# A float32 sum of exponentials split into two fp16 parts, and the second head group normed two bursts sooner, in a fused attention and feed-forward kernel

## The chip, the cores and the metric

One core of one Trainium2 chip runs the whole program in one launch. The metric is the device time of that launch in microseconds (us), the median of several runs. A separate profiled execution gives the trace that all durations below come from. Engines are named as the profile names them: PE is TensorE's matrix multiply and PEld its weight load, DVE is VectorE, ACT is ScalarE, POOL is GpSimd, SP is SyncE, whose queue issues most transfers.

## The reference

The inputs are `q`, `k`, `v` of 8 batches x 12 heads x 448 rows x 64 columns, gains `g_q`, `g_k` of 64, a first weight of 768 x 2048, a second of 2048 x 768 and an `alpha` of 2048, all float32.

```python
def rmsnorm(x, g):
    rms = np.sqrt(np.mean(x * x, axis=-1, keepdims=True) + 1e-06)
    return x / rms * g
q_n, k_n = (rmsnorm(q, g_q), rmsnorm(k, g_k))
scores = scale * np.matmul(q_n, k_n.transpose(0, 1, 3, 2))   # scale = 1/8
attn = softmax(scores)                                       # over the keys
x = np.matmul(attn, v)      # heads put side by side: 3584 x 768
h = x @ w_in
g = np.maximum(h, 0.0) + alpha * np.minimum(h, 0.0)
out = g @ w_out             # 3584 x 768, float32
```

## The kernel before

**Groups and tiles.** The 12 heads of a batch are worked in three groups of four; `y` counts the 24 groups, so that `y % 3` is 0, 1, 2 for the first, second and third group of a batch (`G` is 3). The 448 rows are held as 64 partitions x 7 (`J`) for two halves of the heads.

**Norming a group** takes these steps, each on its own engine: `load_qk` (L100, four transfers of 224 KB on SP's queue), `square` (L144, two POOL instructions), `reduce` (L158, two on DVE), `root` (L167, a logarithm and an exponential on ACT), `scale` (L176, two POOL instructions that write `qs` in fp16, four buffers), `turn_dma` (L274, two transposing transfers on SP's queue, from `qs` to `qT` and `kT`, used from `y = 7` on, `TD`), and `turn` (L284), which for these groups is one DVE instruction (L288) that multiplies the transposed `kT` by the gains in place. It therefore waits for the transfer that wrote `kT`.

**Attention.** `score` (L322) and `soft` (L340) make one key tile's scores on PE and their exponentials on ACT. The sum over the keys comes in two ways. For the first two groups of a batch `den` (L376) sums on PE with a matrix of fp16 ones. For the third group, from `y = 8` on (`pre`, `PRE`), `add_up` (L348) adds the seven exponential tiles on POOL into the float32 tile `rden`, six additions that follow one another, and `den_pre` (L383) sums that tile over partitions with float32 matmuls by `ones32` into two banks `dnb` (L389), which DVE copies back (L397). `log_pre` and `invert` turn it into a reciprocal on ACT; `attv` (L412) multiplies by the values into `av` and DVE scales the result into `xT` (L439).

**Feed-forward.** `up` (L473) is six matmuls into a bank `hT`, a scaled copy `ah` on ACT (L494) and a maximum on DVE into `gT` (L498), which also frees the bank. `down` (L500) is sixteen matmuls into `op` and a copy on DVE (L520). `bank` (L442) gives them one of two banks of the pool `psf`, or, where `spare` is set, the only tile of the pool `psa` (tag `acc`), and then the names are `hTa` and `opa`. The same `psa` tile holds `dn` and `av`; the same `psf` banks hold `dnb`.

**Order.** All of it is written out by hand as 69 bursts (`n`). A burst has two to four key tiles, at most one `den` and one `attv`, and then its `gaps`: the `up` and `down` units that a planner has put there by estimated costs. Every engine takes its instructions in the order of the program. These tables place the norming steps of group `y`: `turn_at[y]` the burst of `turn`; from a burst `n` worked out at L605 to L634 come the loads (`n - 5` or so), the squares (end of `n - 2`), the reduces (`jobs[n]`, inside the gaps) and `roots[n + 1] = y`, where `root`, `scale` and `turn_dma` stand (L844 to L858). A `turn` in a burst whose first gap is an `up` is put ahead of all gaps of the burst (L886); otherwise it follows the `down`. `load_qk` of a burst stands at the burst's start, ahead of everything else. A new tile waits until the last reader of the tile that had its buffer is done; `nat` has six buffers, two for each group.

| burst | tiles of scores | sum and values | gaps | start of its scores, us |
|---|---|---|---|---|
| 24 | (7,6) (8,0) | - | `up` 12, 13, 14 of batch 1 | 102.17 |
| 25 | (8,1) (8,2) (8,3) | `den` of 6, 7 | a `down`, `up` 15 | 106.19 |
| 27 | (9,1) (9,2) | - | a `down` | 119.14 |
| 28 | (9,3) to (9,6) | `den_pre`, `attv` of 8 | two `down` | 122.35 |
| 31 | (10,4) (10,5) | - | `up` 3 to 7 of batch 2 | 140.93 |
| 35 | (12,1) (12,2) | - | `up` 14, 15, a `down` | 166.19 |
| 36 | (12,3) to (12,6) | `den_pre`, `attv` of 11 | two `down` | 172.07 |

Bursts 39, 47 and 55 stand to groups 15, 18 and 21 as burst 31 stands to group 12.

Of the kernel before, what the change touches and what calls it, by code (L numbers as in the profile page):

```python
# [9 lines left out]
FP32 = mybir.dt.float32  # L10
FP16 = mybir.dt.float16
AF = mybir.ActivationFunctionType
ALU = mybir.AluOpType
# [8 lines left out]
def kernel(  # L22
# [12 lines left out]
    nc = tc.nc  # L35

    B, H, S, D = q.shape
# [4 lines left out]
    G = HH // 2  # L42
# [4 lines left out]
    NG = B * G  # L47
    FB = DF // 4
    TD = min(7, NG)
    EB = 3  # L50
    EARLY = 3 * G
    PRE = 3 * G - 1
    assert G == 3

    cst = ctx.enter_context(tc.tile_pool(name="cst", bufs=1))
    ld = ctx.enter_context(tc.tile_pool(name="ld", bufs=2))
# [18 lines left out]
    nc.vector.memset(epsb, RMS_EPS)  # L75
    ones = cst.tile([128, 64], FP16, name="ones", tag="ones")
    nc.vector.memset(ones, 1.0)
    ones32 = cst.tile([128, 64], FP32, name="ones32", tag="ones32")
    nc.vector.memset(ones32, 1.0)
    ident = cst.tile([128, 128], FP16, name="ident", tag="ident")  # L80
    make_identity(nc, ident)
    ident32 = cst.tile([32, 32], FP32, name="ident32", tag="ident32")
# [13 lines left out]
    nat, sqs, qs, ss_t, rr_t, qkT, vt, xT = {}, {}, {}, {}, {}, {}, {}, {}  # L96
# [187 lines left out]
    def turn(y):  # L284

        if y >= TD:
            t = qkT[y, "k"].rearrange("p j g c -> p (j g c)")
            nc.vector.tensor_scalar(  # L288
                out=t, in0=t, scalar1=gain[:, 0:1], scalar2=None, op0=ALU.mult
            )  # L290
            return
        if y <= G:
            ps = [psf.tile([128, 512], FP32, name="tps", tag="mm") for _ in "qk"]
        else:
            ps2 = psa.tile([128, 2, 512], FP32, name="tps2", tag="acc")
            ps = [ps2[:, 0], ps2[:, 1]]
        tps = [
            t[:, : S].bitcast(FP16).rearrange("p (j c) -> p j c", j=J) for t in ps
        ]
        for tp, nm in zip(tps, "qk"):  # L300
            for j in range(J):
                nc.tensor.transpose(
                    tp[:, j, :], qs[y, nm][:, j].rearrange("p h d -> p (h d)"), ident
                )
        for tp, nm in zip(tps, "qk"):
            t = att.tile([128, J, 2, 64], FP16, name=f"{nm}T", tag=f"{nm}T", bufs=4)
            o = t.rearrange("p j g c -> p j (g c)")
            if nm == "q":
                nc.vector.tensor_copy(out=o, in_=tp)
            else:  # L310
                nc.vector.tensor_scalar(
                    out=o, in0=tp, scalar1=gain[:, 0:1], scalar2=None, op0=ALU.mult
                )
            qkT[y, nm] = t


    expT, rden, scs = {}, {}, {}

    def pre(ys):
        return len(ys) == 1 and ys[0] >= PRE and ys[0] % G == G - 1  # L320
# [27 lines left out]
    def add_up(y, j):  # L348
# [6 lines left out]
        s = rden[y,]  # L355
        nc.gpsimd.tensor_add(out=s, in0=e[:, 0] if j == 1 else s, in1=e[:, j])  # L356

    def over_keys(accs, ys, weights):

        m = 64 if len(ys) == 1 and ys[0] < EARLY else 32  # L360
        if len(ys) == 2:
            heads = [(y, par, 0) for y in ys for par in range(2)]
        else:
            heads = [(ys[0], par, c) for par in range(2) for c in range(64 // m)]
        for j in range(J):
            for h, (y, par, c) in enumerate(heads):
                for g in range(2):
                    nc.tensor.matmul(  # L368
                        out=accs[g][ds(m * h, m), :S],
                        lhsT=weights(g, y, par, ts(c, m), j),  # L370
                        rhs=expT[y][ds(64 * g, 64), j, par, :],
                        start=(j == 0),
                        stop=(j == J - 1),
                    )
# [8 lines left out]
    def den_pre(ys):  # L383
        y = ys[0]
        m = 64 if y < EARLY else 32
        accs = [psf.tile([128, 512], FP32, name="dnb", tag="mm") for _ in range(2)]
        for h in range(128 // m):
            for g in range(2):
                nc.tensor.matmul(  # L389
                    out=accs[g][ds(m * h, m), :S],  # L390
                    lhsT=ones32[ds(64 * g, 64), :m],
                    rhs=rden[ys][ds(64 * g, 64), h * m // 64, :],
                    start=True,
                    stop=True,
                )
        for g in range(2):
            nc.vector.tensor_copy(out=rden[ys][:, g], in_=accs[g][:, :S])  # L397

# [134 lines left out]
    def spin(count, wide=True):  # L533

        ps = psf.tile([128, 512], FP32, name="spin", tag="mm")
        for _ in range(count):
            nc.tensor.matmul(
                out=ps[:, :S], lhsT=idle32[:, :128] if wide else ident,
                rhs=idle32 if wide else idle, start=True, stop=True,
            )  # L540
# [4 lines left out]
    bursts, dens, avs, first_in, last_in = [], {}, {}, {}, {}  # L545
    den_at, av_at, split = {}, {}, {}
# [4 lines left out]
    m = 0  # L551
    while m < NG * J or steps:
        n = len(bursts)
        while steps:
            ys, values = steps[0]
# [18 lines left out]
        while len(bursts[n]) < limit and m < NG * J:  # L574
            y, j = divmod(m, J)
# [13 lines left out]
    def at(n, f, *a):  # L589
        prep.setdefault(max(int(n), 0), []).append((f, a))  # L590

    def after(n, f, *a):
        post.setdefault(max(int(n), 0), []).append((f, a))

    turn_at = {
        y: max(n for n in range(first_in[y]) if y >= TD or n not in dens)
        for y in range(1, NG)
    }
    turn_at[2], turn_at[G] = 5, av_at[0]
    turn_at.update(  # L600
        (y, den_at[y - 2] - pre((y - 2,))) for y in range(TD, NG) if y % G == 1
    )
    turns = {n: y for y, n in turn_at.items()}
    jobs = {}
    for y in range(G, NG):  # L605

        early = y < G + 2
        if early:
            n = turn_at[y - 1] + 1
        elif y == G + 2:  # L610
            n = den_at[G - 1]
        elif y == 2 * G:
            n = turn_at[y] - 4
        elif y % G == 1:
            n = den_at[y - 4] - 1 - pre((y - 2,))
        elif y % G:
            n = den_at[y - G] - pre((y - G,))
        else:
            n = av_at[y - 4]
        if y in (3 * G - 1, 3 * G):  # L620

            after(den_at[G] - (y < 3 * G), load_qk, y)
        else:
            at(n - (6 if early or y % G == G - 1 and pre((y - G,)) else 3 if y == 2 * G else 4 if y < 3 * G else 5), load_qk, y)
        for nm in "qk":
            if y != 2 * G:
                after(n - 2 - (y % G == G - 1 and pre((y - G,))), square, y, nm)
            if early:
                after(n, reduce, y, nm, (0, 1) if (y, nm) == (G, "k") else None)
            else:  # L630
                jobs.setdefault(n + (y == G + 2 and nm == "k"), []).append((reduce, (y, nm)))
        if y == 3 * G:
            after(n, *jobs[n].pop()[:1], y, "k")
        roots[n + 1 + (y in (G + 2, 3 * G))] = y  # L634
# [31 lines left out]
    gaps = [[] for _ in range(NB)]  # L666
    for b in range(B - 1):
        lo, hi = av_at[G * b + G - 1], av_at[G * b + 2 * G - 1]
        ups, old, new = (list(u) for u in periods[b])
        mlp = sum(u[0] for u in ups + old + new)  # L670
        stop = hi
# [62 lines left out]
    both, full, lo, hi = slice(0, 2), slice(0, J), slice(0, K0), slice(K0, J)  # L734
    for h in range(2):
        part_square("q", slice(h, h + 1), full, nc.scalar)
    for h in range(2):
# [13 lines left out]
        out=gain, in0=cols[:, NF : NF + 1], in1=cols[:, NF + 1 : NF + 2]  # L751
# [30 lines left out]
    for n in range(NB):  # L782
# [41 lines left out]
        if sums:  # L824
            den_pre(dens[n])
            attv(avs[n], 0, False, (log_pre, invert))
        elif n in dens and not lead:
            den(dens[n])
# [15 lines left out]
        if n in roots:  # L844
            y = roots[n]
# [21 lines left out]
        spare_at, clock = [], 0.0  # L867
# [15 lines left out]
        if turned and not ups_first and turns[n] >= TD:  # L883
            jobs.setdefault(n, []).append((turn, (turns[n],)))
        elif turned:
            turn(turns[n])  # L886
        for k, (f, a) in enumerate(gaps[n]):
            spare = k in spare_at
            if f is down:
                down(*a, jobs.pop(n, ()), spare)  # L890
            else:
                f(*a, spare)
                done += 1
                if n in jobs and not (lead and done < 5) and (
                    n < av_at[2 * G - 1] or done % 2
                ):
                    g, c = jobs[n].pop(0)
                    g(*c)
                    if not jobs[n]:
                        del jobs[n]  # L900
                while late and done == late[0][0]:
                    _, g, c = late.pop(0)
                    g(*c)
        if not gaps[n] and n in turns and turns[n] >= G:
            if n < den_at[0]:
                spin(1)
            turn(turns[n])
# [41 lines left out]
```

## Time and profile before

| what | value |
|---|---|
| median of 3 runs | 427.19 us (427.19 to 427.2) |
| the profiled execution | 427.42 us |
| its span, first to last instruction | 425.6 us |
| PE busy | 413.7 us, 97% of the span |
| ACT, POOL, DVE busy | 275.3, 239.4, 222.4 us (65%, 56%, 52%) |
| granted TensorE clock | full (1.0) over the span |
| transfers | 53.36 MB, 125 GB/s on average |

The profiled execution lies 0.23 us above the median, and 1.8 us of its time lie outside the span. A PE that is 97% busy leaves few places where it waits, so most of the time that PE gains or loses shows in the end; what the other engines do counts where PE comes to wait for it.

### The profile page before, as it was taken

What the parts mean: (1) busy time and instruction counts of PE and PEld (TensorE: products, weight loads), DVE (VectorE), ACT (ScalarE), POOL (GpSimd) and SP (SyncE); (2) the same over time, 40 slices, a digit from 0 to 9 for tenths busy, and PEclk for the clock granted to TensorE, in tenths of its full rate; (3) what the DMA queues carried; (4) which work ended last, traced back from release to release, by engine and by line L of the source; (5) the groups of instructions that cost most, each with busy time, mean ns of one, the idle gap of its engine ahead of it and who ended that gap; (6) DMA issues with size and microseconds to landing.
All of it is one profiled execution on the core that took longest, in us unless ns stands there. A gap on an engine that the chain in (4) does not pass through costs nothing.

```text
span 425.6 us, 11138 instructions
## 1 busy us (share of the span) xinstructions
PE 413.7 (97%) x4755; PEld 216.5 (51%) x4755; DVE 222.4 (52%) x331; ACT 275.3 (65%) x384; POOL 239.4 (56%) x173
## 2 busy tenths in 40 slices
PE   7889999999999999999999999999999999999996
PEld 3344454544455454544555545554555445555554
DVE  4875964456454636636564545647453343343421
ACT  5898887778856686578846677668847575332200
POOL 6789993494997299373984479482973009000000
PEclk9999999999999999999999999999999999999999
DMA  8999999999538965568455963545333500111033
GB/s 199 242 240 224 204 195 204 204 195 238 117 73 131 210 102 126 85 158 168 97 104 109 187 148 106 105 103 126 62 55 85 104 2 22 39 37 39 18 76 75
DMA packets 68529, 53.36 MB, mean 125 GB/s; under 512 B 35568, under 2 KB 68480, under 8 KB 68480
## 3 DMA queue, kind: packets, MB, share of 16 engines
q1 hardware_dynamic: 53680, 39.73, 42.5%
q0 software_dynamic: 13984, 11.81, 18.5%
q10 hardware_dynamic: 816, 1.11, 1.0%
q8 instruction: 37, 0.61, 0.6%
q14 instruction: 12, 0.10, 0.1%
HBM read 45.62 MB, written 11.01 MB: 133 GB/s over the span
## 4 chain that ended last, share of the span: by engine, by line
PE 86%; ACT 5%; DVE 4%; POOL 2%; issue 1%; ACTq 1%; POOLq 0%
PE op L508 29%; PE hT L454 21%; PE hTa L454 9%; PE sc L329 8%; PE opa L508 6%; PE av L368 5%; PE dn L368 3%; ACT expT L343 2%; PE avb L368 2%; PE dnb L389 2%; ACT ah L494 2%; DVE gT L498 1%; POOL sq L155 1%; DVE ss L163 1%; ACTq L108 1%
## 5 line engine op out<-in xcount | busy, mean ns | idle before, releaser
L343 ACT ACTIVATE expT<-sc,expb 128x896 f16<-128x896 f32 x168 | 161.3, 1003 | 42.8 <-PE sc L329 42.6
L508 PE MATMUL op<-w_out_sb,gT 128*128 128x384 f16 (+1 forms) x752 | 125.8, 323 | 0.5 <-DVE gT L498 0.5
L508 PEld LDWEIGHTS <-gT 128*128 128x128 f16 x912 | 86.0, 98 | 64.7 <-issue 11.8
L454 PE MATMUL hT<-xT,w_in_sb 128*128 128x448 f16 x552 | 114.7, 353 | 0.8 <-DVE gT L498 0.5
L179 POOL TENSOR_TENSOR qs<-nat,rr 128x896 f16<-128x896 f32 x41 | 68.4, 1690 | 82.4 <-issue 45.6
L454 PEld LDWEIGHTS <-w_in_sb 128*128 128x128 f16 x768 | 73.2, 98 | 73.8 <-issue 9.4
L494 ACT ACTIVATE ah<-hT,cols 128x448 f16<-128x448 f32 x91 | 57.4, 632 | 46.5 <-PE hT L454 45.6
L498 DVE TENSOR_TENSOR gT<-hT,ah 128x448 f16<-128x448 f32 x92 | 57.3, 623 | 50.7 <-ACT ah L494 49.8
L155 POOL TENSOR_TENSOR sq<-nat 128x896 f32<-128x896 f32 (+1 forms) x47 | 75.5, 1625 | 7.9 <-DMA nat<-in_q_dram 7.3
L520 DVE COPY osb<-op 128x384 f32<-128x384 f32 (+1 forms) x47 | 25.7, 548 | 69.3 <-PE op L508 68.9
L329 PE MATMUL sc<-qT,kT 64*32 64x448 f16 (+1 forms) x1092 | 54.0, 356 | 4.4 <-ACT expT L343 2.2
L356 POOL TENSOR_TENSOR rden<-rden,expT 128x896 f32<-128x896 f32 x30 | 56.8, 1895 | 2.4
L163 DVE TENSOR_REDUCE ss<-sq 128x14 f32<-128x896 f32 (+1 forms) x48 | 48.9, 1039 | 1.9 <-POOL sq L155 1.8
L454 PE MATMUL hTa<-xT,w_in_sb 128*128 128x448 f16 x204 | 44.1, 352 | 0.0
L494 ACT ACTIVATE ah<-hTa,cols 128x448 f16<-128x448 f32 x34 | 21.6, 634 | 21.0 <-PE hTa L454 20.9
L329 PEld LDWEIGHTS <-kT 64*32 64x32 f16 (+1 forms) x1092 | 17.0, 93 | 35.7 <-issue 29.3
L498 DVE TENSOR_TENSOR gT<-hTa,ah 128x448 f16<-128x448 f32 x34 | 21.2, 624 | 19.6 <-ACT ah L494 18.9
L439 DVE TENSOR_TENSOR xT<-av,rden 128x896 f16<-128x896 f32 x16 | 17.5, 1091 | 21.5 <-ACT rden L410 15.4
L368 PEld LDWEIGHTS <-vt 64*32 64x32 f16 (+1 forms) x1260 | 21.4, 94 | 12.7 <-issue 2.5
L508 PE MATMUL opa<-w_out_sb,gT 128*128 128x384 f16 x160 | 27.7, 326 | 0.0
L368 PE MATMUL av<-expT,vt 64*32 64x448 f16 (+1 forms) x812 | 26.6, 349 | 0.0
L356 POOL TENSOR_TENSOR rden<-expT 128x896 f32<-128x896 f16 x6 | 11.3, 1878 | 20.9 <-ACT expT L343 20.9
(67 smaller groups left out, 215.8 us busy)
## 6 DMA issues: line engine op xcount, KB each, us to landing
out_dram<-osb SPq DMA_DIRECT2D x109, 96.0 KB, 2.2
nat<-in_q_dram SPq DMA_DIRECT2D x46, 224.0 KB, 4.3
nat<-in_k_dram SPq DMA_DIRECT2D x46, 224.0 KB, 4.8
vt<-in_v_dram POOLq DMA_DIRECT2D x16, 336.0 KB, 5.9
w_in_sb<-in_moe_w_in_dram POOLq DMA_DIRECT2D x12, 256.0 KB, 7.2
w_out_sb<-in_moe_w_out_dram POOLq DMA_DIRECT2D x4, 768.0 KB, 11.1
nat<-in_q_dram ACTq DMA_DIRECT2D x2, 224.0 KB, 4.3
nat<-in_k_dram ACTq DMA_DIRECT2D x2, 224.0 KB, 5.7
```

The source lines that it names most:

```text
L155: nc.gpsimd.tensor_mul(out=sqf[:, c], in0=src[:, c], in1=src[:, c])
L163: nc.vector.tensor_reduce(out=o[:, c], in_=sqs[y, nm][:, c], axis=AXIS_X, op=ALU.add)
L179: eng.tensor_mul(out=t.rearrange("p j h d -> p h j d"), in0=nat[y, nm], in1=rr_t[y][:, "qk".index(nm)].unsqueeze(3).broadcast_to((128, 2, ...
L329: nc.tensor.matmul(out=sc[ds(64 * g + m * c, m), par, :S].rearrange("p (j c) -> p j c", j=J), lhsT=kT[ds(64 * par, 64), j, g, ts(c, m)], r ...
L343: nc.scalar.activation(out=expT[y][:, j], in_=scs[y, j][:, :, :S], func=AF.Exp, scale=QK_SCALE, bias=expb[:, 0:1],)
L356: nc.gpsimd.tensor_add(out=s, in0=e[:, 0] if j == 1 else s, in1=e[:, j])
L368: nc.tensor.matmul(out=accs[g][ds(m * h, m), :S], lhsT=weights(g, y, par, ts(c, m), j), rhs=expT[y][ds(64 * g, 64), j, par, :], start=(j = ...
L454: nc.tensor.matmul(out=hT[:, :S], lhsT=w_in_sb[:, g * G + i, ts(ft, 128)], rhs=xT[b][:, g, i, :], start=(i == 0 and g == 0), stop=(i == G ...
L494: nc.scalar.activation(out=ah, in_=hT[:, :S], func=AF.Copy, scale=alpha_sb[:, ft : ft + 1])
L498: nc.vector.tensor_max(out=gT[:, ft, ds((b & 1) * S, S)], in0=hT[:, :S], in1=ah)
L508: nc.tensor.matmul(out=ops[c][:, :PW], lhsT=gT[:, ft, ts(t, 128)], rhs=w_out_sb[:, ft, ds(oh * OH + c * PW, PW)], start=(ft == 0), stop=(f ...
L520: nc.vector.tensor_copy(out=o[:, ts(c, PW)], in_=ops[c][:, :PW])
```

## The change

Two things change.

**The sum.** `split_sum` is new. In the burst ahead of `den_pre`, after the first unit of the gaps, ACT writes an eighth of the float32 sum as fp16 (`hi`), and DVE writes the rest, an eighth of the sum less `hi`, as fp16 (`lo`). Both take buffers of `qs`. `den_pre` then runs two passes of fp16 matmuls by a matrix of eights, one over `hi`, one over `lo`, into the same banks. The last unit of the gaps in that burst, and no other, is made spare.

**The norming.** For the second group of a batch from `y = 13` on, loads, squares, reduces, root, scale and transposing transfers stand two bursts sooner. The turns of the groups from `y = 10` on move as well.

| group | root, scale, `turn_dma`: before, after | `turn`: before, after |
|---|---|---|
| 10 | 24, 24 | 27, 24 |
| 11 | 28, 28 | 31, 30 |
| 12 | 29, 29 | 33, 31 |
| 13 | 32, 30 | 35, 32 |

The loads of group 13 move from the start of burst 26 to that of burst 24. Groups 14 to 22 repeat this, eight bursts on for each batch: 14, 17, 20 as 11; 15, 18, 21 as 12; 16, 19, 22 as 13. Group 23 keeps its place.

```diff
-    ones32 = cst.tile([128, 64], FP32, name="ones32", tag="ones32")
-    nc.vector.memset(ones32, 1.0)
+    eights = cst.tile([128, 64], FP16, name="eights", tag="eights")
+    nc.vector.memset(eights, 8.0)
...
+    def split_sum(y):
+
+        s = rden[y,]
+        hi, lo = (
+            ld.tile([128, 2, S], FP16, name="qs", tag="qs", bufs=4) for _ in range(2)
+        )
+        nc.scalar.activation(out=hi, in_=s, func=AF.Copy, scale=0.125)
+        nc.vector.scalar_tensor_tensor(
+            out=lo, in0=s, scalar=0.125, in1=hi, op0=ALU.mult, op1=ALU.subtract
+        )
+        halves[y] = (hi, lo)
...
-        for h in range(128 // m):
-            for g in range(2):
-                nc.tensor.matmul(
-                    out=accs[g][ds(m * h, m), :S],
-                    lhsT=ones32[ds(64 * g, 64), :m],
-                    rhs=rden[ys][ds(64 * g, 64), h * m // 64, :],
-                    start=True,
-                    stop=True,
-                )
+        for n, part in enumerate(halves[y]):
+            for h in range(128 // m):
+                for g in range(2):
+                    nc.tensor.matmul(
+                        out=accs[g][ds(m * h, m), :S],
+                        lhsT=eights[ds(64 * g, 64), :m],
+                        rhs=part[ds(64 * g, 64), h * m // 64, :],
+                        start=(n == 0),
+                        stop=(n == 1),
+                    )
...
-    turn_at.update(
-        (y, den_at[y - 2] - pre((y - 2,))) for y in range(TD, NG) if y % G == 1
-    )
+    turn_at.update((y, den_at[y - 2]) for y in range(TD, NG) if y % G == 1)
+    for y in range(PRE + 1, NG):
+        if y - 2 >= PRE and y % G == 1:
+            turn_at[y] = den_at[y - 4] - 1
+        elif y - 1 > PRE and y % G == 0:
+            turn_at[y] = turn_at[y - 1]
+            turn_at[y - 1] -= 1
...
-            n = den_at[y - 4] - 1 - pre((y - 2,))
+            n = den_at[y - 4] - 1 - pre((y - 2,)) - 2 * pre((y - 5,))
...
+        if n + 1 in dens and pre(dens[n + 1]) and gaps[n]:
+            spare_at = [len(gaps[n]) - 1]
         for k, (f, a) in enumerate(gaps[n]):
...
+            if k == 0 and n + 1 in dens and pre(dens[n + 1]):
+                split_sum(dens[n + 1][0])
```

More of the change, by code (lines that the diff above doesn't have):

```diff
@@ L314, in turn @@
             qkT[y, nm] = t
-    expT, rden, scs = {}, {}, {}
+    expT, rden, scs, halves = {}, {}, {}, {}
     def pre(ys):
```

## The prediction

> **What bounds the kernel now.** I read the page's busy shares first, then the chain that ended last, then the waits around the two moved things. PE is the bound and the chain is almost all PE:
>
> ```profile
> PE 413.7 (97%) x4755; PEld 216.5 (51%) x4755; DVE 222.4 (52%) x331; ACT 275.3 (65%) x384; POOL 239.4 (56%) x173
> ...
> PE 86%; ACT 5%; DVE 4%; POOL 2%; issue 1%; ACTq 1%; POOLq 0%
> ```
>
> So whatever takes PE's time or makes PE wait shows in the end. The groups of `den_pre` (by line and shape) and the waits of its tile say what the sum costs now:
>
> ```profile
> L389 PE MATMUL dnb<-rden,ones 64*32 64x448 f32 x80 | 6.9, 547 | 0.0
> ...
>   DVE osb L520: 1.5, 5
>   POOL rden L356: 0.4, 1
> ```
>
> Each of 44 float32 matmuls stands as two records. PE waited 1.5 us there for `osb` copies that freed the banks, and once 0.4 us for POOL's last addition. That is all the sum can give back. The other half of the change moves `turn`, a DVE instruction that waits for a transfer. Groups 10 and 12 show what that transfer stands behind. First group 10: POOL's `scale`, SP's queue, then DVE and PE (timelines of each, starts in us):
>
> ```profile
> 104.40 3.33 POOL L179 TENSOR_TENSOR qs<-nat,rr 128x896 f16<-128x896 f32 x2 [6.32 <-issue]
> ...
> 96.13 1.28 SPq L108 DMA_DIRECT2D nat<-in_k_dram  x2
> 97.53 1.25 SPq L277 DMA_TRANSPOSE qT<-qs  x1
> 98.87 1.24 SPq L277 DMA_TRANSPOSE kT<-qs  x1
> ...
> 106.12 1.24 SPq L277 DMA_TRANSPOSE qT<-qs  x1
> 107.77 1.22 SPq L277 DMA_TRANSPOSE kT<-qs  x1
> ...
> 103.34 0.61 DVE L498 TENSOR_TENSOR gT<-hT,ah 128x448 f16<-128x448 f32 x1
> 104.83 0.62 DVE L498 TENSOR_TENSOR gT<-hT,ah 128x448 f16<-128x448 f32 x1 [0.87 <-ACT ah L494]
> 106.25 0.62 DVE L498 TENSOR_TENSOR gT<-hTa,ah 128x448 f16<-128x448 f32 x1 [0.80 <-ACT ah L494]
> ...
> 106.93 1.52 PE L368 MATMUL dn<-expT,ones 64*32 64x448 f16 x56 [0.17 <-DVE gT L498]
> ```
>
> The reader sees that `qs` of group 10 is ready at 106.08 (q) and 107.73 (k), its transposes go out at once, and PE's `dn` starts when DVE has freed the `psa` tile that `hTa` held. Then group 12, burst 31, SP, DVE and PE again:
>
> ```profile
> 142.21 1.24 SPq L277 DMA_TRANSPOSE kT<-qs  x1
> ...
> DMA to landing us min/median/max: 4.1/4.2/4.3
> ...
> 143.45 0.62 DVE L498 TENSOR_TENSOR gT<-hT,ah 128x448 f16<-128x448 f32 x1 [0.76 <-ACT ah L494]
> ...
> 144.85 2.43 PE L454 MATMUL hT<-xT,w_in_sb 128*128 128x448 f16 x12
> ```
>
> Its `kT` lands at 142.21 + 4.3 = 146.5, after burst 31 has begun (140.93).
>
> **Stall A, group 10.** Its root, scale and transposes stay in burst 24, but its `turn` now stands in burst 24 too, ahead of that burst's three `gT` (`up` 12, 13, 14), because the first gap is an `up`. DVE takes its queue in order, so after 103.96 it waits for `kT`. And group 13's loads now stand ahead of group 10's transposes on SP: they take over group 10's `nat` buffers, so the q loads wait until 106.08, are issued in 1.34, the k loads wait until 107.73 and end about 109.05. The transposes follow at 109.1 and 110.45 (spacing 1.34, as at 97.53 and 98.87). Landing: the pair at 97.53 also stood right behind four loads and took 4.2 to 4.7; the bounds of the trace for other pairs are 2.9 (nothing ahead) and 5.8 (group 8). I take 4.3: 114.75. Then `turn`, 0.44 to 1.12 by the L288 rows, the longer where POOL adds beside it; take 0.7. Then two `gT` of 0.62, the second of which frees `hTa`: 116.7. Queued behind the waiting instruction are three `gT`; PE waits for the second at `dn`, having done `up` 12 to 14 and two scores. Stall: 116.8 - 106.93 = 9.9; bounds 8.2 (landing 2.9, turn 0.44) to 11.7 (5.8, 1.12).
>
> **The clock after stall A.** The trace has no idle PE that long in its middle. At its start PE runs at half pace (a weight load each 0.37) from 1.61 to 6.25; at its end 3.8 us of idle show full clock:
>
> ```profile
> 5.88 0.15 PEld L537 LDWEIGHTS <-ident 128*128 128x128 f16 x1 [0.22 <-issue]
> 6.25 0.67 PEld L537 LDWEIGHTS <-ident 128*128 128x128 f16 x4 [0.22 <-issue]
> ...
> 421.80:425.60 3.80, 0.00 (x1) 0.00 (x0) 0.36 (x1) 0.00 (x0) 0.00 (x0) 1.00 0.24 52
> ```
>
> So the cost lies between 0 and 2.3 (half of 4.64). I take 1.8, nearer the start's row, since 9.9 is far over 3.8. [...]
>
> **Stall B, groups 12, 15, 18, 21.** Their transposes keep their place; their `turn` comes two bursts sooner, ahead of the five `up` of bursts 31, 39, 47, 55. DVE then waits until `kT` has landed, runs 0.44 (POOL rests there) and only then the first `gT` (0.62), which frees the bank for the fourth `up` (PE adds 0.06). Burst 31: 146.5 + 0.5 + 0.62 + 0.06 = 147.68 against 144.85, so 2.8. Likewise with `kT` issued at 191.19, 239.68, 288.94 and landing 3.6, 4.4, 3.8 later, and the fourth `up` at 194.13, 243.05, 292.33: 1.85, 2.2, 1.6. Sum 8.4; bounds 6.4 and 11.0 with landings 0.5 either way and a `turn` of up to 0.6 more at POOL's side. Groups 11, 14, 17, 20 follow a `down`, or land before their burst (14: 182.79 + 2.9 = 185.7 against 186.45), and cost nothing. Groups 13, 16, 19, 22 have their transposes two bursts sooner, behind the earlier ones (13: issued about 146.0, landed 150.3, wanted at 149.9 + 2.8): nothing, covered by stall B itself; were B absent, some 1 us each.
>
> **The sum.** Float32 takes, from the last score to `av`, 0.81 in group 8 without its wait, 0.95 in groups 11 to 20 with the wait for `osb`, and 1.50 in the last. Two fp16 passes take 0.39 (as 8 score matmuls 64*64) or 0.44 (16 of 64*32; 72 such run in 2.0, 173.40 to 175.41). New on ACT: `hi`, 0.95 by the L401 row, hidden in its idle ahead of `den_pre` (3.9 us at 221.12). New on DVE: `lo`, no such row; 0.87 (fp16 L288, with POOL) to 1.09 (float32 L179); take 1.09, its input being float32.
> - Groups 14, 20 (two `down`): both covered, the spare bank ends the wait: -0.5 each.
> - Groups 11, 17: `split_sum` sits between two `up`. `ah` 15 moves behind `hi` (169.6 to 170.55), `gT` 15 behind `lo` (170.6 to 171.7), done 172.3. The `down` starts 0.25 sooner but its sixteenth matmul needs `gT` 15 at 171.57: 0.8 lost, 0.25 and 0.5 gained: about 0.
> - Group 8: one `down`, so `lo` stands behind the `osb` copy: `av` 2.0 after the scores instead of 1.31, and the spare tile is still being copied, 0.2: +0.9.
> - Group 23: the third `up` loses its spare bank (0.4), `den_pre` falls from 1.50 to 0.44: -0.65.
>
> Together -0.65; bounds -4.4 (all of the float32 excess, 3.6, and every wait, 0.8, gone) and +2 (the loss of group 8 in 11 and 17 as well).
>
> **Sum.** 427.42 + 9.9 + 1.8 + 8.4 - 0.65 = 446.9 for a profiled execution, 0.2 less as a median (427.19 against 427.42): 446.6.
>
> **Rivals.**
> 1. Only stall A: B is hidden, if the transposes of group 12 leave SP at least 3 us sooner. SP's row is packed from 131.76 to 144.8, which speaks against. 427.2 + 9.9 + 1.8 - 0.65 = 438.3.
> 2. Only stall B: group 10's `turn` finds `kT` in time. `qs` ends at 107.73, so it can't. 434.9.
> 3. The change does what its words say, with neither stall: the float32 excess and the waits go. 427.2 - 0.65 to -4.4: 423 to 426.5, faster. The place is the DVE queue in burst 24, the price what A and B sum to; it decides if that is under 0.65. Against it: the data for `kT` does not exist at 103.96.
> 4. Worse: SP's queue, held up by loads that wait for POOL, delays later loads and squares by a burst in each batch, 5 x 2 us more: 457. The free time of POOL (8.8 us before `scale` at 149.45) speaks against.
>
> **How the numbers follow.** Main case 0.80, rival 1 0.08, rival 2 0.03, rival 3 0.06, rival 4 0.03. Low ends together: 427.2 + 8.2 + 0 + 6.4 - 4.4 = 437.4; high ends: 427.2 + 11.7 + 2.3 + 11.0 + 2 = 454.2. They will not all fall together, so 437 to 453, which takes in rival 1. About 0.2% (0.85 us) can be told from no change: faster 0.06, same 0.02, slower 0.92.
>
> **What would show it.** Right: a DVE wait of some 10 us at L288 in burst 24, PE idle before `dn` L368 of about 10 us, PEclk below 1.0 after it; four PE waits of 1.5 to 3 us at `hT` put down to DVE; `dnb` near 0.45 a group. Wrong: PE's idle before `dn` under 1 us, or no PE wait in bursts 31, 39, 47, 55.

## The result and the profile after

The changed kernel takes 447.78 us, the median of 6 runs (446.36 to 449.74), against 427.19 before (427.17 to 428.08): a ratio of 1.0481, 95% interval 1.0455 to 1.0507. The prediction was 446.6, range 437 to 453. The profiled execution took 448.82 with a span of 446.9.

The page of the changed kernel first: busy shares, granted clock in 40 slices of 11.2 us, and the chain that ended last.

```profile
PE 415.6 (93%) x4755; PEld 214.9 (48%) x4755; DVE 225.3 (50%) x337; ACT 280.2 (63%) x390; POOL 243.0 (54%) x173
...
PEclk9899999999699999999999969999999999999999
...
PE 74%; ACT 6%; DVE 5%; issue 5%; DMA 5%; POOL 4%; SPq 1%; ACTq 1%; POOLq 0%; DVEq 0%
```

PE is busy 415.6 us against 413.7, but its share of the chain is 74% against 86%: most of the 21.3 us of new span is time in which PE waits. The clock has two dips in its middle, slices 11 and 24, and one at its start, slice 2, ahead of anything that the change moves. The waits of the changed kernel name what came last (total us, times, longest):

```profile
DVE kT L288 <- DMA kT<-qs: 23.4, 5, 9.9
...
PE dn L380 <- DVE gT L511: 9.4, 1, 9.4
PE hT L467 <- DVE gT L511: 7.7, 7, 3.1
...
PE dnb L402 <- DVE qs L365: 1.0, 1, 1.0
```

Five times DVE stood at `turn` (L288) for a transfer of `kT`; once that held `dn`, four times an `up`. The last row is PE waiting for `lo` (L365) in group 8. Stall A, the timelines of SP, DVE and PE and the clock (the column before the last two of a windows row):

```profile
106.84 1.25 SPq L108 DMA_DIRECT2D nat<-in_q_dram  x2
108.48 1.25 SPq L108 DMA_DIRECT2D nat<-in_k_dram  x2
109.83 1.25 SPq L277 DMA_TRANSPOSE qT<-qs  x1
111.13 1.30 SPq L277 DMA_TRANSPOSE kT<-qs  x1
...
114.56 1.21 DVE L288 TENSOR_SCALAR kT<-kT,gain 128x896 f16<-128x896 f16 x1 [9.87 <-DMA kT<-qs]
...
116.88 2.81 PE L380 MATMUL dn<-expT,ones 64*32 64x448 f16 x56 [9.40 <-DVE gT L511]
...
112.00:116.00 4.00, 0.00 (x0) 0.00 (x0) 1.45 (x2) 0.00 (x0) 3.44 (x2) 0.50 0.61 112
116.00:120.00 4.00, 3.12 (x60) 1.23 (x59) 1.36 (x3) 0.00 (x0) 0.00 (x0) 0.50 0.01 4
```

Group 13's loads stand ahead of group 10's transposes, `turn` waits 9.87 us, and `dn` starts after 9.40 us of idle; the clock is then half. The fence below is burst 47, DVE, PE and clock:

```profile
260.32 0.45 DVE L288 TENSOR_SCALAR kT<-kT,gain 128x896 f16<-128x896 f16 x1 [4.71 <-DMA kT<-qs]
...
261.36 4.64 PE L467 MATMUL hT<-xT,w_in_sb 128*128 128x448 f16 x12 [3.06 <-DVE gT L511]
...
262.00:264.00 2.00, 2.00 (x7) 0.81 (x6) 0.36 (x1) 0.21 (x1) 0.00 (x0) 0.50 0.63 123
264.00:266.00 2.00, 2.00 (x14) 0.59 (x20) 0.62 (x1) 0.43 (x1) 0.00 (x0) 0.50 0.99 253
```

The idle is 3.06 us, and then twelve matmuls take 4.64 where twelve such took 2.43 before: the clock fell here too.

To place every microsecond I subtract, burst by burst, the start of the burst's first score matmul in the trace of before from that in another trace, and take the steps of this difference. Each row holds the steps that belong to one cause, in us; the columns after the first are experiments told below (sooner = the schedule of the change).

| place | changed | float sum, sooner | group 10 back | groups 12-21 back | both back | split only |
|---|---|---|---|---|---|---|
| 24 to 26, stall A | 10.92 | 10.64 | 0.00 | 11.78 | 0.01 | 0.01 |
| 28, 29, sum of group 8 | 0.74 | 0.00 | 6.11 | 0.75 | 6.07 | 6.25 |
| 32, turn of group 12 | 1.69 | 2.19 | 0.00 | 0.00 | 0.00 | 0.00 |
| 36, 37, sum of group 11 | 0.24 | 0.00 | 0.24 | 0.25 | 0.27 | 0.63 |
| 40, turn of group 15 | 1.56 | 1.68 | 1.92 | 0.00 | 0.00 | 0.00 |
| 45, sum of group 14 | -0.61 | 0.00 | -0.61 | -0.61 | -0.61 | -0.08 |
| 48, 49, turn of group 18 | 5.86 | 2.43 | 2.72 | -0.19 | -0.19 | 0.00 |
| 52, 53, sum of group 17 | 0.24 | 0.00 | 0.24 | 0.25 | 0.26 | 0.63 |
| 56, turn of group 21 | 1.16 | 1.34 | 1.01 | 0.00 | 0.00 | 0.00 |
| 61, sum of group 20 | -0.61 | 0.00 | -0.61 | -0.61 | -0.61 | -0.61 |
| after 66, sum of group 23 | -0.38 | 0.00 | -0.39 | -0.37 | -0.39 | -0.37 |

The changed column sums to 20.8. A step of +0.94 in its first 17 us, ahead of anything that the change moves, and -0.4 in bursts 20 and 33, which "float sum, sooner" shows too, make it the 21.3 of the spans. The +0.94 goes with the clock dip of slice 2, which the profiled executions of before, "group 10 back" and "split only" do not have, so it is no part of the change. The profiled execution of "both back" has two such dips in its first 26 us, together +1.88.

### The profile page after: what moved, and what is told of

Read it like the earlier page. It is cut to its first block, busy times and chain, and to the rows that moved or that the text cites. A ratio compares the mean times of both kernels' runs of the same rounds, so it can differ in the third digit from the quotient of the medians.

```text
span 446.9 us, 11155 instructions
## 1 busy us (share of the span) xinstructions
PE 415.6 (93%) x4755; PEld 214.9 (48%) x4755; DVE 225.3 (50%) x337; ACT 280.2 (63%) x390; POOL 243.0 (54%) x173
## 4 chain that ended last, share of the span: by engine, by line
PE 74%; ACT 6%; DVE 5%; issue 5%; DMA 5%; POOL 4%; SPq 1%; ACTq 1%; POOLq 0%; DVEq 0%
PE op L521 23%; PE hT L467 17%; PE opa L521 8%; PE sc L329 7%; PE hTa L467 6%; PE av L380 5%; DMA kT<-qs 5%; POOL qs L179 3%; PE dn L380 3%; ACT expT L343 3%; PE avb L380 2%; DVE gT L511 1%; ACT ah L507 1%; DVE osb L533 1%; PE spin L550 1%
## 5 line engine op out<-in xcount | busy, mean ns | idle before, releaser
L467 PE MATMUL hT<-xT,w_in_sb 128*128 128x448 f16 x558 | 118.8, 358 | 7.7 <-DVE gT L511 7.7
L467 PEld LDWEIGHTS <-w_in_sb 128*128 128x128 f16 x768 | 73.6, 99 | 83.5 <-issue 20.8
L521 PE MATMUL op<-w_out_sb,gT 128*128 128x384 f16 (+1 forms) x656 | 109.7, 323 | 0.0
L155 POOL TENSOR_TENSOR sq<-nat 128x896 f32<-128x896 f32 (+1 forms) x47 | 78.6, 1691 | 10.3 <-DMA nat<-in_q_dram 4.3
L533 DVE COPY osb<-op 128x384 f32<-128x384 f32 (+1 forms) x41 | 22.4, 546 | 61.4 <-PE op L521 61.4
L521 PE MATMUL opa<-w_out_sb,gT 128*128 128x384 f16 x256 | 44.6, 326 | 1.7 <-DVE gT L511 1.6
L467 PE MATMUL hTa<-xT,w_in_sb 128*128 128x448 f16 x198 | 42.8, 352 | 0.0
L329 PEld LDWEIGHTS <-kT 64*32 64x32 f16 (+1 forms) x1092 | 16.1, 93 | 36.7 <-issue 30.4
L380 PEld LDWEIGHTS <-vt 64*32 64x32 f16 (+1 forms) x1260 | 19.5, 93 | 13.1 <-issue 2.8
L380 PE MATMUL dn<-expT,ones 64*32 64x448 f16 (+1 forms) x504 | 16.4, 374 | 9.6 <-DVE gT L511 9.4
```

The costliest lines, as they stand in the source:

```text
L155: nc.gpsimd.tensor_mul(out=sqf[:, c], in0=src[:, c], in1=src[:, c])
L329: nc.tensor.matmul(out=sc[ds(64 * g + m * c, m), par, :S].rearrange("p (j c) -> p j c", j=J), lhsT=kT[ds(64 * par, 64), j, g, ts(c, m)], r ...
L380: nc.tensor.matmul(out=accs[g][ds(m * h, m), :S], lhsT=weights(g, y, par, ts(c, m), j), rhs=expT[y][ds(64 * g, 64), j, par, :], start=(j = ...
L467: nc.tensor.matmul(out=hT[:, :S], lhsT=w_in_sb[:, g * G + i, ts(ft, 128)], rhs=xT[b][:, g, i, :], start=(i == 0 and g == 0), stop=(i == G ...
L521: nc.tensor.matmul(out=ops[c][:, :PW], lhsT=gT[:, ft, ts(t, 128)], rhs=w_out_sb[:, ft, ds(oh * OH + c * PW, PW)], start=(ft == 0), stop=(f ...
L533: nc.vector.tensor_copy(out=o[:, ts(c, PW)], in_=ops[c][:, :PW])
```

## The experiments

The theory was that stall A, stall B and the sum are three separate prices that add up. The rivals: one of the stalls is all of it; the split alone is a gain (rival 3); SP's queue is the cause. Four kernels undo the parts.

**Group 10's turn alone back.** The edit, ahead of where `turns` is made from `turn_at`:

```diff
+    turn_at[10] = 27
     turns = {n: y for y, n in turn_at.items()}
```

> The changed kernel with the turn of group 10 alone back in burst 27, where it stood before; its transposes, all other turns and the split sum stay as changed. Theory (stall A and stall B are separate and add): the start of burst 26 no longer comes 10.9 us late, so 447.8 - 10.9 = 436.9, 436 to 438.2; full clock from 108 to 124 us, but the four waits of bursts 31, 39, 47 and 55 unchanged (together about 10 us with the clock after burst 47). Rival, A is all of it and the other waits only follow from it: 426.5 to 428. Rival, the late transposes of group 10 cost wherever the turn stands: over 440, with a wait of 3 us or more at dn or at the scores of group 10.

Measured: 437.83 us (437.25 to 440.26), ratio 1.0245 (1.0221 to 1.0269). The number is near the theory's, but the table says that the theory is wrong: stall A is gone (0.00), burst 32 lost its stall as well, burst 47 costs 2.7 and not 5.9, and 6.1 us have appeared in group 8, which cost 0.74 in the changed kernel. These terms hang together: while PE loses its time in group 8, SP's queue goes on, so that `kT` of group 12 is issued at 145.05, 1.9 us ahead of burst 31 (146.96); in the changed kernel it is issued at 153.86, 0.5 us after burst 31 has begun (153.31). A total that fits is no proof of its terms.

**The turns of groups 12, 15, 18 and 21 alone back.**

```diff
+    for y in range(12, 22, 3):
+        turn_at[y] += 2
     turns = {n: y for y, n in turn_at.items()}
```

> The changed kernel with the turns of groups 12, 15, 18 and 21 alone two bursts later, in bursts 33, 41, 49 and 57 as before; group 10 and the split sum stay as changed. Theory with the clock: the four idles (1.52, 1.40, 3.06, 1.00 = 7.0 us) and the lower clock after burst 47 (about 2.8 us) go, 447.8 - 9.8 = 438.0, and the granted clock is 1.0 after 130 us. Theory without the clock (the slow stretch after burst 47 has another cause): 440.8, with the clock still down near 260 us. My prediction said for this case that the sooner transposes of groups 13, 16, 19 and 22 then cost some 1 us each: 442. Rival, only B matters: 426 to 428.

Measured: 438.76 us (437.83 to 439.38), ratio 1.0254 (1.0238 to 1.027). All four stalls are 0, and no clock dip is left after stall A's (the twelve `hT` matmuls of burst 47 take 2.43 us). This is the theory with the clock: the median is 9.0 below the changed kernel's, more than the 7.0 of plain idle. The 9.8 expected is missed by about what stall A takes more in this trace, 11.78 against 10.92, after the same idle of 9.40. The sooner transposes of groups 13, 16, 19 and 22, for which the prediction had some 1 us each in this case, cost nothing.

**Both back (e3_both_back), and the split alone (e4_split_only).** The first takes the two edits above together. The second takes neither: it has the whole schedule of before (its `turn_at` and its load bursts), so that only the split is left of the change:

```diff
-    turn_at.update((y, den_at[y - 2]) for y in range(TD, NG) if y % G == 1)
-    for y in range(PRE + 1, NG):
-        ...
+    turn_at.update(
+        (y, den_at[y - 2] - pre((y - 2,))) for y in range(TD, NG) if y % G == 1
+    )
...
-            n = den_at[y - 4] - 1 - pre((y - 2,)) - 2 * pre((y - 5,))
+            n = den_at[y - 4] - 1 - pre((y - 2,))
```

> The changed kernel with both of these undone: the turn of group 10 in burst 27, those of groups 12, 15, 18 and 21 in bursts 33, 41, 49 and 57; groups 11, 13, 14, 16 and so on are still normed and turned sooner, and the sum is split. Theory: what is left is the split sum, +0.74 (group 8), +0.24 each (11, 17), -0.61 each (14, 20) and -0.38 (23) = -0.4, so 426.8, 426 to 427.6. The prediction's remark on groups 13, 16, 19 and 22 (some 1 us each once stall B is absent): 430.8. Rival 3 (the float32 excess and its waits all go): 423 to 424.

> The split sum alone: every load, root, transpose and turn stands in the burst where it stood before, only the float32 sum is split in two fp16 parts as in the change. Theory: -0.4 by the steps seen in the changed kernel's trace (my prediction's sum: -0.65), so 426.5 to 427. Rival 3: 423 to 424, if the 3.6 us of float32 excess all lie on the path. Rival, slower: group 8's and groups 11's and 17's losses without the gains, 428 to 428.5. Also tells whether the sooner norming is worth anything by itself, beside the kernel with both turns back.

Measured: 431.26 us (429.18 to 433.63), ratio 1.0071 (1.0051 to 1.0091), and 433.37 us (432.88 to 434.07), ratio 1.0131 (1.0116 to 1.0146). Every version of the theory falls, and rival 3 too: without the stalls the split is no gain, it is 3.4 and 5.5 us slower than the runs of before beside it (427.86), and the one large step, 6.1 to 6.2, stands in group 8. That 431.26 lies near the 430.8 of the prediction's remark on groups 13, 16, 19 and 22 is chance: no step in the table is theirs. (The profiled execution of "both back", 433.63, is the slowest of its six.) The split alone, POOL, ACT, DVE, PE and clock there, and last POOL and ACT of the changed kernel:

```profile
112.74 9.80 POOL L356 TENSOR_TENSOR rden<-rden,expT 128x896 f32<-128x896 f32 x5
122.49 3.46 POOL L155 TENSOR_TENSOR sq<-nat 128x896 f32<-128x896 f32 x2
...
122.57 0.95 ACT L364 ACTIVATE qs<-rden 128x896 f16<-128x896 f32 x1 [1.26 <-POOL rden L356]
...
122.94 1.49 DVE L288 TENSOR_SCALAR kT<-kT,gain 128x896 f16<-128x896 f16 x1
124.34 2.56 DVE L365 SCALAR_TENSOR_TENSOR qs<-rden,qs 128x896 f16<-128x896 f32 x1
...
123.57 0.38 PE L402 MATMUL dnb<-qs,eights 64*64 64x448 f16 x4 [0.65 <-ACT qs L364]
126.96 0.59 PE L402 MATMUL dnb<-qs,eights 64*64 64x448 f16 x4 [3.00 <-DVE qs L365]
...
130.97 6.26 PE L521 MATMUL op<-w_out_sb,gT 128*128 128x384 f16 x32
...
126.00:130.00 4.00, 3.04 (x32) 1.56 (x31) 2.06 (x3) 1.13 (x2) 1.26 (x2) 0.50 0.71 101
...
125.95 5.82 POOL L356 TENSOR_TENSOR rden<-rden,expT 128x896 f32<-128x896 f32 x3 [2.65 <-ACT expT L343]
...
133.03 0.95 ACT L364 ACTIVATE qs<-rden 128x896 f16<-128x896 f32 x1
```

Group 10's `turn` stands in burst 27 again, ahead of `lo`, and both run beside POOL's squares of group 12: `turn` takes 1.49 and `lo` 2.56, where they take 0.44 and 1.08 with POOL at rest. PE waits 0.65 and 3.00, the clock halves, and 32 `op` matmuls take 6.26 us against the 5.38 of before. In the changed kernel group 8 pays only 0.97 of waiting. One reason is that `turn` has left this burst. The other is POOL: here its additions for group 8 end at 122.54, just as PE ends its scores (122.92), and `hi` waits for them. In the changed kernel PE stood in stall A and POOL caught up, so that the additions end at 131.77 and `hi` is made at 133.03, ahead of PE's `dnb` at 134.69. No run takes the second reason alone. So the parts don't add: what makes stall A is also what keeps the split cheap.

**The sooner schedule alone**, with the float32 sum of before in `den_pre`, no `split_sum` and no unit made spare for it, tests the same from the other side:

```diff
-        for n, part in enumerate(halves[y]):
-            for h in range(128 // m):
-                ...
+        for h in range(128 // m):
+            for g in range(2):
+                nc.tensor.matmul(
+                    out=accs[g][ds(m * h, m), :S],
+                    lhsT=ones32[ds(64 * g, 64), :m],
+                    rhs=rden[ys][ds(64 * g, 64), h * m // 64, :],
+                    start=True,
+                    stop=True,
+                )
...
-                split_sum(dens[n + 1][0])
```

> The other half of the change alone: all loads, roots, transposes and turns stand where the change puts them, the sum of every third group stays in float32 as before. Theory (the split is worth little where group 10's turn has left burst 27; stall A and stall B are the whole of the loss): without the split's steps (+0.74 in group 8, +0.24 each in 11 and 17, -0.61 each in 14 and 20, -0.38 in 23 = -0.4) 447.8 + 0.4 = 448.2, 447 to 449. Rival (the 6 us that the split costs on the schedule of before are there in the changed kernel too, hidden in the sum): 447.8 - 6.2 = 441.6.

Measured: 446.38 us (445.22 to 447.3), ratio 1.044 (1.0419 to 1.046). The rival (441.6) is out: on the sooner schedule the split costs 1.4 us between medians, not 6.2. The theory's 448.2 is missed by 1.8 the other way; in the profiled runs the largest part of that is burst 47, where `hT` waited 2.46 and the clock stayed up, 2.43 against 5.86 in the table. So the 1.4 is not the price of the split: its own steps in the changed column sum to -0.4, and the rest is how the stalls and the clock fell.

**Group 8 alone in float32**, on the schedule of before (all other groups split as in the change; the matrices of ones and eights are 32 columns wide, so that group 8's sum takes two blocks of 32 and not one of 64). `split_sum` is called, and `spare_at` set, only where `halved` holds:

```diff
+        halved = n + 1 in dens and pre(dens[n + 1]) and dens[n + 1][0] > PRE
...
-        for n, part in enumerate(halves[y]):
+        parts = halves.get(y, (rden[ys],))
+        for n, part in enumerate(parts):
```

> The split alone (e4_split_only) with one thing undone: group 8's sum stays in float32. Groups 11 and 17 are split behind the first up as in the change. Theory (group 8 carries all of the loss of the split alone): 433.4 - 6.0 = 427.4, 427 to 428, with a step of +0.1 in bursts 28 and 29; groups 11 and 17 +0.6 each, 14 and 20 0 to -0.6 each, 23 -0.4. Rival (the split costs by itself in every group): above 429.

Measured: 427.75 us (427.55 to 428.66), ratio 1.0003 (0.9993 to 1.0014), 5.6 below the split alone. Group 8 carried all the loss. What is left is no gain either: +0.6 each in groups 11 and 17 eats what groups 20 and 23 give.

**SP's part of stall A.** The changed kernel, but with group 13's loads in burst 26 again:

```diff
-            at(n - (6 if early
+            at(26 if y == 13 else n - (6 if early
```

> The changed kernel with one thing undone: the loads of group 13 are issued in burst 26 again, not in burst 24. The turn of group 10 stays in burst 24. Theory (a part of stall A is SP's queue: the four loads that wait for the buffers of group 10 push its transposes back by 2.9 us): kT of group 10 is issued near 108.5 instead of 111.13 and lands 2.9 to 4.3 later, so the idle before dn falls from 9.4 to 6.0, 5.5 to 7.5; the clock still drops after it; 447.8 - 3.4 = 444.4, 443.5 to 446. Rival, POOL's scale alone sets it (the loads go out beside the transposes at no cost): unchanged, 447 to 448.

Measured: 443.45 us (441.09 to 444.01), ratio 1.0351 (1.0326 to 1.0376).

```profile
108.46 1.22 SPq L277 DMA_TRANSPOSE kT<-qs  x1
...
113.07 2.82 PE L380 MATMUL dn<-expT,ones 64*32 64x448 f16 x56 [5.62 <-DVE gT L511]
```

`kT` goes out 2.67 us sooner and the idle falls from 9.40 to 5.62. So 3.8 of stall A came from the loads that stood ahead on SP: 2.7 by the later issue, 0.5 by a longer landing (3.4 against 2.9) and 0.6 by `turn`, which takes 0.58 here and 1.21 in the changed kernel, beside an addition on POOL. 5.6 remain with nothing of theirs ahead, since the transposes still have to wait for POOL's `scale`.

**The order on DVE.** The split alone again, with group 10's `turn` behind `lo`, at the end of burst 27:

```diff
     turns = {n: y for y, n in turn_at.items()}
+    del turns[27]
...
         for _, g, c in late:
             g(*c)
+        if n == 27:
+            turn(10)
```

> The split alone (the kernel of e4_split_only), with the turn of group 10 moved from ahead of the split of group 8 to the end of burst 27, behind it. In e4_split_only the difference of 6 us arose here: lo (2.56 us beside POOL's square) stood behind that turn (1.49), PE waited 0.65 and then 3.00 for it, and then ran 32 op matmuls in 6.26 instead of 5.38, at a lower clock. Theory with the clock: lo starts when hi ends (123.5) and, if it again takes 2.56 beside POOL, ends at 126.1; PE's idle is about 2.1 and not 3.0, so the clock stays up, and the step in bursts 28 and 29 is 2.8 to 3.5 instead of 6.05: 430.4, 430 to 431.5. With a lo of 1.3 (the length of most others) 429. Rival, the clock drops after 2 us of idle too: 432. Rival, the order on DVE is not the cause: 433.4.

Measured: 431.0 us (430.7 to 431.38), ratio 1.0079 (1.0065 to 1.0092), 2.4 below the split alone.

```profile
123.76 0.38 PE L402 MATMUL dnb<-qs,eights 64*64 64x448 f16 x4 [0.65 <-ACT qs L364]
125.36 0.38 PE L402 MATMUL dnb<-qs,eights 64*64 64x448 f16 x4 [1.22 <-DVE qs L365]
...
128.69 5.76 PE L521 MATMUL op<-w_out_sb,gT 128*128 128x384 f16 x32
...
126.00:128.00 2.00, 2.00 (x32) 0.96 (x32) 2.00 (x3) 0.00 (x0) 2.00 (x3) 0.53 0.03 8
```

The order was a cause: the longer wait falls from 3.00 to 1.22 (`lo` took 1.57). But the clock fell even so, after only 1.87 us of idle in two pieces, so that neither of my two numbers was right for its own reason: the step is 3.3, within the theory's bounds, with a shorter idle and a clock loss that the theory had left out. Nor is the order all: the changed kernel pays 0.74 here, and the 0.65 for `hi`, which waits for POOL's last addition, is still there.

**Where the split may stand.** Two kernels (e6_float_in_group8 and e7_float_in_group8_sooner) keep group 8 in float32 as above and, in groups 11 and 17, call `split_sum` behind the second `up` of the burst and not the first. The first is on the schedule of before, the second on the one with both turns back:

```diff
+        two_ups = halved and len(gaps[n]) == 3
...
+                if halved and two_ups and k == 1:
+                    split_sum(dens[n + 1][0])
...
-            if k == 0 and n + 1 in dens and pre(dens[n + 1]):
+            if halved and k == 0 and not two_ups:
                 split_sum(dens[n + 1][0])
```

> The schedule of before; group 8's sum stays in float32 (two column blocks of 32 instead of one of 64), the sums of groups 11, 14, 17, 20 and 23 are split, and in groups 11 and 17 the split stands behind the second up of its burst instead of the first. Theory: no 6 us in group 8; -0.1 (group 8 at the most +0.15), -0.6 each in groups 14 and 20, -0.4 in group 23, and 0 to -0.5 each in groups 11 and 17 in place of +0.6: 427.2 - 1.6 to - 2.6 = 425.6 to 424.6. If the split behind the second up makes dnb wait for lo instead: up to +0.8 each, 427.2.

> As e6_float_in_group8, on the schedule with both turns back (e3_both_back): groups 11, 14, 17 and 20 turned one burst sooner, groups 13, 16, 19 and 22 normed two bursts sooner. Theory: what e6_float_in_group8 shows, less the 0.2 us at each of bursts 33 and 49 that e3_both_back and the changed kernel showed: 0.4 us below it, 424.2 to 425.2. Rival, sooner norming costs by itself (group 13's and later loads ahead of transposes): above e6_float_in_group8.

Measured: 427.06 us (426.67 to 428.51), ratio 0.9994 (0.9984 to 1.0004), no difference that can be told; and 428.76 us (428.12 to 430.57), ratio 1.0032 (1.0017 to 1.0046). Both are above the theory. On the schedule of before, DVE and PE in group 11:

```profile
172.16 1.19 DVE L367 SCALAR_TENSOR_TENSOR qs<-rden,qs 128x896 f16<-128x896 f32 x1
173.27 1.07 DVE L165 TENSOR_REDUCE ss<-sq 128x14 f32<-128x896 f32 x1
174.27 0.54 DVE L536 COPY osb<-opa 128x384 f32<-128x384 f32 x1
...
174.86 1.52 PE L382 MATMUL av<-expT,vt 64*32 64x448 f16 x56 [1.06 <-DVE osb L536]
```

`dnb` finds `lo` in time, but `av` waits 1.06 us for the bank that the `osb` copy frees, and that copy stands behind `lo` and a `reduce` that nobody waits for yet. On the sooner schedule `lo` of the same group meets POOL again:

```profile
167.38 4.96 POOL L157 TENSOR_TENSOR sq<-nat 128x896 f32<-128x896 f32 x3
...
170.83 2.45 DVE L367 SCALAR_TENSOR_TENSOR qs<-rden,qs 128x896 f16<-128x896 f32 x1
...
173.33 0.38 PE L405 MATMUL dnb<-qs,eights 64*32 64x448 f16 x8 [1.05 <-DVE qs L367]
174.79 2.81 PE L382 MATMUL av<-expT,vt 64*32 64x448 f16 x56 [1.08 <-DVE osb L536]
```

Here norming sooner is itself harmful: it puts the first square of group 16, the third in that row, beside `lo`.

**A version that beats both.** As e6_float_in_group8, with the second `reduce` of bursts 35 and 51 behind the `osb` copy:

```diff
         two_ups = halved and len(gaps[n]) == 3
+        if two_ups and n in jobs:
+            post.setdefault(n, []).insert(0, jobs[n].pop())
```

> As e6_float_in_group8, and the second reduce of bursts 35 and 51 stands behind the osb copy of the burst's down instead of ahead of it, so that the copy frees the bank for av 1 us sooner. Theory: the wait of av for osb, 1.06 and 1.07 in groups 11 and 17, goes to about 0.15, 427.06 - 1.8 = 425.2, 424.9 to 425.8. Rival (the dnb copy, now behind the reduce as before, or the reduce itself is late for its root): 427.

Measured: 424.73 us (424.59 to 425.78), ratio 0.9934 (0.9918 to 0.995) to before. Group 11 in its DVE and PE timelines, and from the waits of the tile `dnb`:

```profile
171.10 1.19 DVE L367 SCALAR_TENSOR_TENSOR qs<-rden,qs 128x896 f16<-128x896 f32 x1
172.21 0.54 DVE L536 COPY osb<-opa 128x384 f32<-128x384 f32 x1
172.68 1.07 DVE L165 TENSOR_REDUCE ss<-sq 128x14 f32<-128x896 f32 x1
...
172.81 1.52 PE L382 MATMUL av<-expT,vt 64*32 64x448 f16 x56
...
  DVE osb L536: 0.2, 1
```

`av` no longer waits. The steps are -0.9 each in groups 11 and 17, -0.6 in group 20, -0.4 in group 23 and +0.1 in group 8: -2.7, which is the difference of the medians. So the split, its spare unit and the later `reduce` are together worth 2.7 us, where `lo` stands clear of POOL and of what PE waits for. How much of it the fp16 passes give is open, as no run has the float32 sum with the same spare unit and `reduce`: the waits of `dnb` for `osb` copies alone, 1.5 us before, are 0.2 here.

## Why the prediction was right, point by point

- **Stall A**: 9.9 predicted, 9.40 measured. The issue of `kT` was right: 111.13, less the 0.72 by which this trace is already late there (the +0.94 of its start and -0.22 of burst 20), is 110.41, against 110.45. Two errors offset each other in part: it landed 3.4 later, not 4.3, and `turn` took 1.21, not 0.7. Two bounds had been read too narrow: the L288 rows of before go up to 1.90 and not 1.12, and the landings up to 8.0 (group 7) and not 5.8. That SP's loads were part of it was argued, and is now shown (3.8 us).
- **The clock after stall A**: 1.8 predicted. From `dn` to the next `up` the changed kernel takes 6.06 us, before 4.37: 1.69. That the size fits is in part luck: after the same idle of 9.40 the drop cost 1.41 in "float sum, sooner" and 2.55 in "groups 12-21 back" (1.69 and the difference of their stall A from the changed kernel's). The row at the end of before, idle at full clock, misled as a lower bound; where PE had work afterwards, all eight idles of 3.00 to 9.40 us in these traces were followed by slowed matmuls, with a clock of 0.50 in the four kernels whose windows rows show it there.
- **Stall B**: 8.4 predicted. The place was right in all four bursts and the idles are 1.52, 1.40, 3.06 and 1.00, together 7.0, where it had 2.8, 1.85, 2.2 and 1.6. The step of the prediction that failed is that it charged the clock to stall A alone: burst 47's idle took it down as well, and cost 5.86 - 3.06 = 2.8 more. In the table stall B comes to 10.3. `kT` of group 18 landed 5.7 us after its issue (the prediction had 4.4), and that made this idle the long one. In "float sum, sooner", where burst 47 kept its clock, the four come to 7.6.
- **The sum**: -0.65 predicted, -0.4 measured (0.74 + 0.24 - 0.61 + 0.24 - 0.61 - 0.38). The prediction's own terms (-0.5, -0.5, 0, +0.9, -0.65) add up to -0.75, a slip of 0.1. Each sign was right but those of groups 11 and 17, set at about 0, which lost 0.24.
- **Rival 3** had the wrong price. It said that without the stalls the change is faster, 423 to 426.5; the kernel with both turns back takes 431.26. The prediction's +0.9 for group 8 held only because group 10's `turn` had left burst 27 and POOL had caught up in stall A, and the text had seen neither. Its duration for `lo`, 1.09, is right only beside a resting POOL (1.08 or 1.09; 1.19 to 2.56 beside squares).
- **Rivals 1 and 2**, only one of the stalls: the changed trace has both, and undoing either takes 9 to 10 us away. **Rival 4**: no step in the table is put down to loads that come a burst late.
- The remark that groups 13, 16, 19 and 22 would cost some 1 us each without stall B was wrong: 0.

The median came out 1.2 above the prediction, the profiled execution 1.9 above the 446.9 given for it. In that trace stall B has 1.9 more, the clock dip at the start 0.9 and the sum 0.3, against 0.8 less in stall A with its clock and 0.4 less in bursts 20 and 33.

## What to carry to other kernels

Before an instruction that waits for a transfer is moved up in an in-order queue, compare the time at which its data can exist with the time at which the queue will reach it; what stands behind it pays the difference (here `turn` waited 9.87 us for `kT`, and PE 9.40 for a `gT` behind it). Prices of two parts of a change add only if neither part moves what the other stands behind: here undoing the costly part made the cheap part cost eight times as much. A few hundred nanoseconds gained on the busiest engine are worth it only if the new work on the other engines is placed clear of what frees its banks (`av` waited 1.06 us for `osb`), and clear of a neighbour that slows it (`lo` took 2.56 us beside POOL's squares and 1.08 without).

## What the runs showed of the hardware

**An idle of 2.73 us took the clock down in one run; one of 2.75 did not in another.** Eight idles of PE of 3.00 to 9.40 us stood ahead of more work: 9.40 and 3.06 in the changed kernel, 9.40 in "float sum, sooner" and "groups 12-21 back", 5.62 with group 13's loads back, 3.01 in "both back", 3.00 in "split only" and "group 10 back". Behind each of them the matmuls were slow: `dn` took 2.81 or 2.82 against 1.52 before, `hT` 4.64 against 2.43, `dnb` 0.59 against 0.38; and the windows rows of four of these kernels (the changed one, "split only", "group 10 back", group 13's loads back) show a clock of 0.50 there. At 2.7 it went both ways, in the same burst 47 of two kernels, group 10's turn back first and then group 13's loads back:

```profile
253.35 2.43 PE L467 MATMUL hT<-xT,w_in_sb 128*128 128x448 f16 x12 [2.75 <-DVE gT L511]
```

```profile
257.42 4.11 PE L467 MATMUL hT<-xT,w_in_sb 128*128 128x448 f16 x12 [2.73 <-DVE gT L511]
```

Idle in pieces took it down too: after 0.65 and 1.22 around a 0.38 us burst of matmuls it was 0.53 from 126 to 128 us, and after 1.05 and 1.08 around such a burst in group 11 of the sooner kernel 0.51 from 176 to 178 us (the `av` of 2.81 us above, against 1.52); but it stayed at 1.00 in that kernel's group 17, after 1.06 and 1.08.

The recorded clock tells these cases apart. In the changed kernel's trace all its changes lie a whole number of 3.41 us apart, at 11.34, 14.75, 110.32, 120.56, 260.51 and 267.33, that is 1, 28, 3, 41 and 2 times 3.413; in that of before the rise at 6.23 and the fall at 426.07 lie 123 times 3.413 apart. So a trace can be cut into such windows. The rows below are windows of three kernels in turn: group 10's turn back and group 13's loads back, both around the idle in burst 47, and `lo` ahead of group 10's `turn`, around the pieces in group 8 (behind the window's length stands PE's busy time; the third number from the end is the clock):

```profile
248.71:252.12 3.41, 1.89 (x11) 0.88 (x9) 0.00 (x0) 2.35 (x4) 2.26 (x2) 1.00 0.94 159
252.12:255.53 3.41, 2.18 (x12) 1.07 (x11) 2.23 (x5) 0.63 (x1) 0.00 (x0) 1.00 0.92 192
...
254.41:257.83 3.42, 0.69 (x5) 0.25 (x4) 1.45 (x4) 0.74 (x2) 1.65 (x1) 1.00 1.20 239
257.83:261.24 3.41, 3.41 (x11) 1.25 (x9) 1.22 (x3) 0.64 (x1) 0.00 (x0) 0.50 0.73 172
...
122.70:126.11 3.41, 1.54 (x36) 0.79 (x24) 2.88 (x3) 2.75 (x3) 3.41 (x3) 1.00 0.25 58
126.11:129.52 3.41, 3.41 (x42) 1.32 (x32) 2.05 (x3) 1.23 (x2) 2.04 (x3) 0.50 0.32 39
```

The idle of 2.75 lies across an edge, 1.52 and 1.23 us, and the clock stays; that of 2.73 lies inside one window, with PE busy for 0.69, and the clock falls at its end. In the changed kernel, from 28 to 441 us, it fell at the end of the two windows with PE busy for 0.57 and 1.20 us, and at that of no other; the least busy of the others at full clock has 2.39. It came back, both times, at the end of a window with PE busy for all of its 3.41 us, and one with 2.56 ahead of that kept it down. In the rows above, windows with 0.69 and 1.54 took it down, and those with 1.89 and 2.18 did not. So these two drops of the changed kernel, at a clock of 0.50, cost about half of the time from PE's return to the edge at which the clock came back: 116.88 to 120.56 for stall A, half of which is 1.84 (1.69 measured), and 261.36 to 267.33 in burst 47, half of which is 2.99 (2.80 measured). Where the edges fall differs from trace to trace: the first rise of the clock comes at 4.51 us in the changed kernel's and at 6.23 in that of before.

**Where DVE's `lo` ran beside a square of POOL, it ended 0.94 to 0.96 us after that square.** In the split alone POOL's squares end at 122.49 + 3.46 = 125.95 and `lo` at 124.34 + 2.56 = 126.90; in the sooner kernel they end at 172.34 and `lo` at 173.28. Four rows of the changed kernel, three of the split alone and one each of e6_float_in_group8 and e7_float_in_group8_sooner show it, with `lo` starting from 1.61 to 0.24 us before the square's end; in the other five rows of the changed kernel and the split alone, where no square runs, it takes 1.08 or 1.09. So its end went with the square's end and not with its own start.
